# Threshold attention and a squared-ReLU layer on one core: thresholds on ScalarE, first loads over two queues, values and results on GpSimd's queue

## The chip, the cores and the metric

The kernel runs on one core of a Trainium2 chip. The metric is device time in microseconds (us); lower is better. Single executions of the kernel before took between 1449.8 and 1459.9 us over the whole study, so kernels are compared by several executions of each, taken in turn on the same chip.

## The reference, cut to what matters

```python
scores = scale * np.matmul(q, k.transpose(0, 1, 3, 2))          # 8 batches x 8 heads, 576 x 64
thresh = np.max(scores, axis=-1, keepdims=True) - tau
scores = np.where(scores >= thresh, scores, -1000000000.0)
attn = softmax(scores)                                            # written out in the reference
x = (attn @ v) laid out as (4608 tokens, 512)
h = x @ w_in;  r = np.maximum(h, 0.0);  out = (r * r) @ w_out     # 512 -> 2048 -> 512, all fp32
```

## The kernel before

The program is recorded in a fixed order for each engine. It walks over 36 "visits" (a pair of heads each) in 160 steps. A step multiplies a block of scores on TensorE (into two score tiles of two banks of TensorE's result memory each, with no second copy, so that VectorE must have read a bank before the next scores go in), takes the row maximum, adds the threshold, exponentiates on ScalarE, masks and sums on VectorE, and divides on GpSimd. The attention weights are then transposed: by TensorE in the first 11 visits, later by VectorE in blocks of 32 and 48 small DMAs per visit (`by_dma`). In between, `fill` deals out pieces of the two layers (`mlp_in`, `product`) of 1.76 us of TensorE work each. A `product` has work that must follow it (additions on VectorE, the store of the result), which is recorded after the next piece.

```python
def load_qk(n):
    for x, t in zip(rows_of(n), (q, k)):
        queue = nc.scalar if n == 0 and t is k else nc.sync
        for m in range(4): ...                      # 4 loads of q, 6 of k, runs of 128 bytes

def load_v(n):
    for u in range(2):                              # 128x4x64 and 64x64 per head
        nc.sync.dma_start(out=t[:, at:at + NBLK, :], in_=...)
        nc.sync.dma_start(out=t[u * D:(u + 1) * D, at + NBLK, :], in_=...)

def scores(s):
    ...                                             # matmuls into sc[u]
    mx, thr = (st[:, j, 0:n] for j in range(2))
    for u in range(n):
        nc.vector.tensor_reduce(out=mx[:, u:u + 1], in_=sc[u][:, :, 0:HALF], axis=AX.XY, op=ALU.max)
    nc.vector.tensor_scalar(out=thr, in0=mx, scalar1=ntau8, scalar2=None, op0=ALU.add)

def exponents(vis, i):
    nc.scalar.activation(out=bias, in_=mx, func=AF.Copy, scale=-SCALE)
    for u in range(len(sc)):
        nc.scalar.activation(out=w[:, u, :]..., in_=sc[u]..., func=AF.Exp, bias=bias[:, u:u + 1], scale=SCALE)

def threshold(vis, i):                              # masks, sums, frees the score banks
    for u in range(n):
        nc.vector.scalar_tensor_tensor(out=wu, in0=sc[u]..., scalar=thr[:, u:u + 1], in1=wu,
                                       op0=ALU.is_ge, op1=ALU.mult, accum_out=sm[:, u:u + 1])
    ...

def place_blocks(vis, pair):                        # 16 issues; three times per visit
    for qb in range(4):
        for j in range(4):
            nc.sync.dma_start(out=to[...], in_=wb[rows, j::4, :, :]...)

def store_rows(j, t0, t1):
    nc.sync.dma_start(out=out[...], in_=osb[:, t0:t1, :])
# ... cuts: rounding of the weights, transposes, the layers, the main loop
```

Of the kernel before, what the change touches and what calls it, by code (L numbers as in the profile page):

```python
# [11 lines left out]
AF = mybir.ActivationFunctionType  # L12
ALU = mybir.AluOpType
# [6 lines left out]
def kernel(  # L20
# [10 lines left out]
    nc = tc.nc  # L31
    B, H, S, D = q.shape
    d_model, d_ff = moe_w_in.shape
    n_tokens = out.shape[0]
    P = 128
    HP = H // 2
    NPAIR = B * HP
    NBLK = S // P
# [18 lines left out]
    ntau8 = const.tile([P, 1], FP32, name="ntau8")  # L57
# [21 lines left out]
    at = RAW * 2 * WP  # L79
# [18 lines left out]
    osb = const.tile([P, 2, d_model], FP32, name="osb")  # L98
# [48 lines left out]
    def rows_of(n):  # L147
        return rows_in[n % 2 if n <= 2 * HP else 0]

    def load_qk(n):  # L150


        b, h = divmod(visits[n][0], HP)
        h *= 2
        for x, t in zip(rows_of(n), (q, k)):
            queue = nc.scalar if n == 0 and t is k else nc.sync
            for m in range(4):
                src = t[b, h + m // 2, :, (m % 2) * 32:(m % 2) * 32 + 32].rearrange("(c p) d -> p c d", p=32)
                last = REST // 32 if t is k and m >= 2 else 0
                to = x[m * 32:(m + 1) * 32, :, :]  # L160
                queue.dma_start(out=to[:, last:, :], in_=src[:, 0:S // 32 - last, :])  # L161
                if last:
                    queue.dma_start(out=to[:, 0:last, :], in_=src[:, S // 32 - last:, :])  # L163

    def load_v(n):
        b, h = divmod(visits[n][0], HP)
        h *= 2
        t = vs[n % 2]
        for u in range(2):
            at = u * (NBLK + 1)  # L170
            nc.sync.dma_start(out=t[:, at:at + NBLK, :],
                              in_=v[b, h + u, 0:NBLK * P, :].rearrange("(c p) d -> p c d", p=P))
            nc.sync.dma_start(out=t[u * D:(u + 1) * D, at + NBLK, :], in_=v[b, h + u, NBLK * P:S, :])

    def prep(n):

# [9 lines left out]
    def scores(s):  # L186

        vis, i = steps[s]
        n = 2 if i < NBLK else 1
        sc = [psum.tile([P, 2, 512], FP32, tag=f"s{u}", name=f"s{u}") for u in range(n)]  # L190
        halves = [(half, u) for half in range(2) for u in range(n)]
        if early():
            halves.sort(key=lambda x: x[1])
        for half, u in halves:
            if i < NBLK:
                rows, lhsT = slice(u * D, (u + 1) * D), qT[u * D:(u + 1) * D, i * P:(i + 1) * P]
            else:
                rows, lhsT = slice(0, P), qmid
            nc.tensor.matmul(sc[u][:, half, 0:HALF], lhsT, kT[rows, half * HALF:(half + 1) * HALF],  # L199
                             start=True, stop=True)  # L200
        st = pool.tile([P, 7, 2], FP32, tag="st", name="st", bufs=4)
        mx, thr = (st[:, j, 0:n] for j in range(2))
        for u in range(n):
            nc.vector.tensor_reduce(out=mx[:, u:u + 1], in_=sc[u][:, :, 0:HALF], axis=AX.XY, op=ALU.max)  # L204
        nc.vector.tensor_scalar(out=thr, in0=mx, scalar1=ntau8, scalar2=None, op0=ALU.add)

        w = w_slots[(s - first_dma) % (2 if by_dma(vis) else 3)][:, 0:n, :]
        weights[vis, i] = w, sc, st

    def exponents(vis, i):  # L210
        w, sc, st = weights[vis, i]
        mx, bias = (st[:, j, 0:len(sc)] for j in (0, 2))
        nc.scalar.activation(out=bias, in_=mx, func=AF.Copy, scale=-SCALE)  # L213
        for u in range(len(sc)):
            nc.scalar.activation(out=w[:, u, :].rearrange("p (h k) -> p h k", h=2), in_=sc[u][:, :, 0:HALF],  # L215
                                 func=AF.Exp, bias=bias[:, u:u + 1], scale=SCALE)
# [174 lines left out]
    def mlp_out(j, f):  # L391

        if f == 0:
            used["o"] = [take("mm", (6, 7)) for t in range(2)]
        o = used["o"]
        for t in range(2):
            mov = wo[:, Q00:Q01 + 1:Q01 - Q00, f, :] if f < HF else wo[:, Q10:Q11 + 1, f - HF, :]
            nc.tensor.matmul(o[t].rearrange("p (h d) -> p h d", h=2), g[:, f, t * P:(t + 1) * P], mov,  # L398
                             start=(f == 0), stop=(f == NFT - 1))
        if f < NFT - 1:  # L400
            return []

        def store():
            for t in range(2):
                nc.scalar.copy(osb[:, t, :], o[t])
            store_rows(j, 0, 2)
        return [store]

    def store_rows(j, t0, t1):
        lo = j * TCH  # L410
        nc.sync.dma_start(out=out[lo + t0 * P:lo + t1 * P, :].rearrange("(t p) d -> p t d", p=P), in_=osb[:, t0:t1, :])



# [2 lines left out]
    def product(j, x, half):  # L417

        if x == 0 and half == 0:
            a, c, b = ring3[2], ring3[0], ring3[1]  # L420
            used["abc"] = a, b, c
            ring3[:] = [b, a, c]
        a, b, c = (bank[y][:, 0:HD] for y in used["abc"])
        p = PRODUCTS[x]
        g0, g1 = g[:, 0:HF, :], g[:, HF:, :]
        left, slot, to = {
            "1": (g0[:, :, 0:P], Q00, a), "5": (gsum[0], FT1, c), "6": (gsum[1], FT2, b), "2": (g1[:, :, 0:P], Q10, a),
            "7": (gsum[0], FT3, b), "4": (g1[:, :, P:], FT4, a), "3": (gsum[1], Q11, c)}[p]
        for f in range(half * HF // 2, (half + 1) * HF // 2):
            nc.tensor.matmul(to, left[:, f, :], wo[:, slot, f, :], start=(f == 0), stop=(f == HF - 1))  # L430
        if not half:
            return []

        def halves(fn):
            for lo in (0, HF // 2):
                fn(slice(lo, lo + HF // 2))

        def then():
            add, sub, tt, u = ALU.add, ALU.subtract, nc.vector.tensor_tensor, u_sum
            if p == "1":  # L440
                nc.scalar.copy(p1s, a)
            elif p == "5":
                halves(lambda f: tt(out=gsum[0][:, f, :], in0=g0[:, f, 0:P], in1=g0[:, f, P:], op=sub))  # L443
            elif p == "6":
                tt(out=u, in0=b, in1=p1s, op=add)  # L445
                tt(out=osb[:, 0, HD:], in0=c, in1=u, op=add)
                halves(lambda f: tt(out=gsum[1][:, f, :], in0=g1[:, f, 0:P], in1=gsum[1][:, f, :], op=sub))
            elif p == "2":
                tt(out=osb[:, 0, 0:HD], in0=a, in1=p1s, op=add)  # L449
            elif p == "7":  # L450
                tt(out=u, in0=b, in1=u, op=add)
                tt(out=osb[:, 1, HD:], in0=c, in1=u, op=add)
            elif p == "4":
                tt(out=osb[:, 1, 0:HD], in0=u, in1=a, op=sub)
                store_rows(j, 1, 2)
            else:
                tt(out=osb[:, 0, HD:], in0=c, in1=osb[:, 0, HD:], op=add)
                store_rows(j, 0, 1)
        return [then]


# [8 lines left out]
    def by_dma(n):  # L470

        return n >= 3 * HP - 1
# [21 lines left out]
    chunk_at, j = {}, 0  # L494
# [3 lines left out]
            j += 1  # L498
    PIECE_US = 1.76
    waiting = deque()  # L500
    state = {"us": 0.0, "left": 0.0, "step": 0, "rounded": 0, "then": []}

    def early():
        return state["step"] < min(chunk_at)
# [24 lines left out]
        return best  # L529

    def after():
        for fn in state["then"]:
            fn()
        state["then"] = []

    def fill(us):
        state["left"] += us
# [10 lines left out]
    pieces, left = [], n_pieces  # L548
    for s, (n, i) in enumerate(steps):
        if s < HP * FIRST:  # L550
            x = int(n > 0 and i == 0)
        else:
            x = 2 if n >= 2 * HP and i == NBLK else 1
# [19 lines left out]
    for s in range(END + 1):  # L573
        state["step"] = s
        on = s < NST
        now = []
        if on:
            n, i = steps[s]
            at = visits[n][1].index(i)
            last = at == len(visits[n][1]) - 1  # L580
            now = list(range(done, done + pieces[s]))
            done += pieces[s]
            more = n + 1 < len(visits)
            short = n < 2 * HP
            if short and at == 0 and 0 < n + 1 < 2 * HP:
                load_qk(n + 2)
            elif not short and at == 1 and more:
                load_qk(n + 1)
            if now:
                round_weights(now[0], 0)  # L590
            scores(s)
# [6 lines left out]
        if on:  # L598
            if at_once:
                exponents(n, i)  # L600
            if lay:
                prep(n + 1)
            elif now:
                round_weights(now[0], 1)
                round_weights(now[0], 2)
# [4 lines left out]
        if 0 < s <= NST and by_dma(steps[s - 1][0]):  # L610
            m, x = steps[s - 1]
# [25 lines left out]
        if on:  # L637
# [8 lines left out]
            elif last and more and n >= 2 * HP:  # L646
                load_v(n + 1)
    after()
    assert not waiting


# [30 lines left out]
```

## Time and profile before

| | before |
|---|---|
| device time, median of 3 | 1455.95 us (1454.76 to 1457.42) |
| the profiled execution | 1450.02 us, span 1448.2 us |
| TensorE busy | 1387.1 us, 96% of the span |
| VectorE / ScalarE / GpSimd busy | 62% / 29% / 43% |
| DMA issues on SyncE's queue | 1,764; full from 290 to 1280 us |

 "Clock" below is the granted clock: the share of TensorE's full speed that the profile shows as allowed; half clock is 0.5.

Names in all views: PE is TensorE, DVE VectorE, ACT ScalarE, POOL GpSimd, SPq SyncE's DMA queue. L199 is a line of the kernel; in the changed kernel most lines have moved by one (L199 to L200, L227 to L228, L318 to L319, L430 to L431).

### The profile page before, as it was taken

To read this page: it belongs to the slowest core of one execution; us is meant where nothing else is said; L and a number is where in the kernel's file an instruction comes from. 1 tells how busy PE (TensorE), PEld (TensorE's weight loads), DVE (VectorE), ACT (ScalarE), POOL (GpSimd) and SP (SyncE) were. 2 spreads that over 40 slices of the span, in tenths; PEclk is the share of its full clock that TensorE was granted. 3 is DMA by queue.
4 is the path that set the end of the run, shared out by engine and by line. 5 is a ranking of instruction groups with operands and counts; after the bars stand their busy time and mean duration, and the time that the engine had idled before them with its cause. 6 is when DMAs were issued, how large, how long until landed. Compare 5 with 4: busy or idle time off the path is not lost.

```text
span 1448.2 us, 22131 instructions
## 1 busy us (share of the span) xinstructions
PE 1387.1 (96%) x7412; PEld 1058.0 (73%) x7412; DVE 904.5 (62%) x1930; ACT 423.1 (29%) x904; POOL 623.9 (43%) x794
## 2 busy tenths in 40 slices
PE   5898888999999999999999999999999999999998
PEld 3676555747787777777777777777777777788887
DVE  5899886568766676666675767666667666631011
ACT  3666554223222322222322222222222222210100
POOL 3588765425343444343343435343434352422321
PEclk9899999999999999999999999999999999999999
DMA  7564442345445545545455454555554445440000
GB/s 149 119 140 109 112 112 52 55 84 96 85 96 91 109 85 96 88 92 88 97 96 105 84 96 85 95 89 100 95 101 84 89 90 91 90 81 19 5 15 15
DMA packets 532528, 125.94 MB, mean 87 GB/s; under 512 B 523712, under 2 KB 523712, under 8 KB 532416
## 3 DMA queue, kind: packets, MB, share of 16 engines
q1 hardware_dynamic: 529984, 124.24, 44.7%
q8 instruction: 60, 0.98, 0.3%
q10 hardware_dynamic: 2400, 0.30, 0.2%
q14 instruction: 52, 0.43, 0.1%
q0 software_dynamic: 32, 0.00, 0.0%
HBM read 48.63 MB, written 9.44 MB: 40 GB/s over the span
## 4 chain that ended last, share of the span: by engine, by line
PE 65%; SPq 20%; DVE 6%; issue 3%; DMA 2%; ACT 2%; POOL 1%; DVEq 0%; ACTq 0%; POOLq 0%
PE bank L367 26%; PE bank L430 16%; SPq L299 12%; PE s L199 9%; PE bank L318 8%; SPq L306 5%; PE bank L398 3%; SPq L161 3%; DVE st L204 2%; PE bank L257 1%; SPq L163 1%; DVE w L227 1%; DVE turned L288 1%; DMA vs<-in_v_dram 1%; DVE turned L138 1%
## 5 line engine op out<-in xcount | busy, mean ns | idle before, releaser
L367 PE MATMUL bank<-xT,w_in_sb 128*128 128x256 f32 x2304 | 519.8, 382 | 3.5 <-POOL w_in_sb L144 2.4
L367 PEld LDWEIGHTS bank<-xT,w_in_sb 128*128 128x128 f32 x2304 | 431.6, 190 | 84.2 <-issue 21.3
L204 DVE TENSOR_REDUCE st<-s 128x1 f32<-128x576 f32 x288 | 206.7, 753 | 296.9 <-PE s L199 296.9
L378 POOL TENSOR_TENSOR g<-g 128x512 f32<-128x512 f32 x144 | 149.8, 1042 | 232.2 <-ACT g L377 209.4
L239 POOL TENSOR_SCALAR w<-w,st 128x576 f32<-128x576 f32 x269 | 236.4, 888 | 31.2 <-DVE st L230 25.2
L227 DVE SCALAR_TENSOR_TENSOR w<-s,st,w 128x576 f32<-128x576 f32 x269 | 207.3, 803 | 52.2 <-ACT w L215 51.9
L430 PE MATMUL bank<-wo,gsum 128*128 128x256 f32 x1024 | 234.2, 382 | 2.9 <-DVE u_sum L445 1.6
L430 PEld LDWEIGHTS bank<-wo,gsum 128*128 128x128 f32 x1024 | 192.5, 190 | 38.6 <-issue 7.6
L199 PE MATMUL s<-kT,qT 64*128 64x288 f32 x1024 | 176.8, 438 | 30.4 <-DVE kT L178 10.3
L237 POOL TENSOR_SCALAR st<-st 128x2 f32<-128x2 f32 (+1 forms) x160 | 38.7, 242 | 379.7 <-DVE w L227 366.1
L215 ACT ACTIVATE w<-s,st 128x576 f32<-128x576 f32 x269 | 186.1, 738 | 12.1 <-ACT st L213 0.4
L318 PE MATMUL bank<-wT,vs 128*64 128x128 f32 (+3 forms) x1700 | 179.7, 358 | 8.7 <-DMA wT<-turned 3.5
L430 PE MATMUL bank<-wo,g 128*128 128x256 f32 x768 | 178.7, 383 | 2.9 <-DVE osb L449 2.9
L199 PEld LDWEIGHTS s<-kT,qT 64*128 64x128 f32 x1024 | 101.1, 190 | 95.2 <-issue 71.4
L288 DVE STREAM_TRANSPOSE turned<-w 128x576 f32<-128x576 f32 x225 | 163.0, 758 | 10.1 <-DMA wT<-turned 3.8
L430 PEld LDWEIGHTS bank<-wo,g 128*128 128x128 f32 x768 | 143.8, 190 | 32.4 <-issue 8.2
L318 PEld LDWEIGHTS bank<-wT,vs 128*64 128x64 f32 x1700 | 107.9, 141 | 78.1 <-issue 25.6
L377 ACT ACTIVATE g<-bank 128x512 f32<-128x512 f32 x144 | 86.3, 599 | 200.7 <-PE bank L367 200.7
L213 ACT ACTIVATE st<-st 128x2 f32<-128x2 f32 (+1 forms) x160 | 33.2, 208 | 328.2 <-DVE st L204 327.5
L332 ACT COPY xT<-bank 128x256 f32<-128x256 f32 x42 | 15.7, 373 | 287.9 <-PE bank L318 287.9
L443 DVE TENSOR_TENSOR gsum<-g 128x512 f32<-128x512 f32 x32 | 20.8, 681 | 107.3 <-PE bank L430 107.3
L398 PE MATMUL bank<-wo,g 128*128 128x512 f32 x128 | 62.0, 619 | 7.3 <-POOL wo L144 7.0
(66 smaller groups left out, 858.1 us busy)
## 6 DMA issues: line engine op xcount, KB each, us to landing
wT<-turned SPq DMA_DIRECT2D x800, 72.0 KB, 2.2
ql<-in_q_dram SPq DMA_DIRECT2D x128, 72.0 KB, 2.5
vs<-in_v_dram SPq DMA_DIRECT2D x72, 128.0 KB, 2.5
wo<-in_moe_w_in_dram SPq DMA_DIRECT2D x16, 512.0 KB, 4.5
wo<-in_moe_w_out_dram SPq DMA_DIRECT2D x16, 512.0 KB, 3.6
out_dram<-osb SPq DMA_DIRECT2D x32, 256.0 KB, 2.3
kl<-in_k_dram SPq DMA_DIRECT2D x62, 72.0 KB, 2.6
wT<-turned SPq DMA_DIRECT2D x200, 20.0 KB, 1.9
```

Of the source, the lines that this page charges most:

```text
L199: nc.tensor.matmul(sc[u][:, half, 0:HALF], lhsT, kT[rows, half * HALF:(half + 1) * HALF], start=True, stop=True)
L204: nc.vector.tensor_reduce(out=mx[:, u:u + 1], in_=sc[u][:, :, 0:HALF], axis=AX.XY, op=ALU.max)
L215: nc.scalar.activation(out=w[:, u, :].rearrange("p (h k) -> p h k", h=2), in_=sc[u][:, :, 0:HALF], func=AF.Exp, bias=bias[:, u:u + 1], sca ...
L227: nc.vector.scalar_tensor_tensor(out=wu, in0=sc[u][:, :, 0:HALF], scalar=thr[:, u:u + 1], in1=wu, op0=ALU.is_ge, op1=ALU.mult, accum_out=s ...
L239: nc.gpsimd.tensor_scalar(out=w[:, u, :], in0=w[:, u, :], scalar1=z[:, u:u + 1], scalar2=rcp[:, u:u + 1], op0=ALU.add, op1=ALU.mult)
L288: nc.vector.transpose(wb[:, u * KB:(u + 1) * KB, i % 2, :], w[:, u, :].rearrange("p (k q) -> p k q", q=32))
L299: nc.sync.dma_start(out=to[:, :, at:at + 64], in_=wb[rows, j::4, :, :].rearrange("p c u q -> p c (u q)"))
L318: nc.tensor.matmul(ps[u * D:(u + 1) * D, 0:nq], vs[n % 2][:, u * (NBLK + 1) + c, :], wT[:, cw, cols], start=(c == 0), stop=(c == NBLK))
L367: nc.tensor.matmul(h[:, x % 2, :], w_in_sb[:, c, f * P:(f + 1) * P], xT[:, c, at:at + TCH], start=(c == 0), stop=(c == NMC - 1))
L378: nc.gpsimd.tensor_tensor(out=to, in0=to, in1=to, op=ALU.mult)
L398: nc.tensor.matmul(o[t].rearrange("p (h d) -> p h d", h=2), g[:, f, t * P:(t + 1) * P], mov, start=(f == 0), stop=(f == NFT - 1))
L430: nc.tensor.matmul(to, left[:, f, :], wo[:, slot, f, :], start=(f == 0), stop=(f == HF - 1))
```

## The change

Intent: to take the threshold addition off VectorE, to get the first q and k in sooner, and to relieve SyncE's queue of the value loads of the DMA-transposed visits and of the results. Results are held back by one piece of work so that GpSimd does not stand waiting for VectorE's additions.

```diff
 def load_qk(n):
-        for x, t in zip(rows_of(n), (q, k)):
-            queue = nc.scalar if n == 0 and t is k else nc.sync
+        for x, t in list(zip(rows_of(n), (q, k)))[::-1]:
             for m in range(4):
+                queue = nc.scalar if n == 0 and m % 2 else nc.sync
 def load_v(n):
+        queue = nc.gpsimd if by_dma(n) else nc.sync
-            nc.sync.dma_start(...)                 # both loads
+            queue.dma_start(...)
 def scores(s):
-        nc.vector.tensor_scalar(out=thr, in0=mx, scalar1=ntau8, scalar2=None, op0=ALU.add)
 def exponents(vis, i):
         nc.scalar.activation(out=bias, in_=mx, func=AF.Copy, scale=-SCALE)
+        nc.scalar.activation(out=thr, in_=mx, func=AF.Identity, bias=ntau8)
 def store_rows(j, t0, t1):
-        nc.sync.dma_start(...)
+        nc.gpsimd.dma_start(...)
 def product(j, x, half):
-                store_rows(j, 1, 2)
+                return [lambda: store_rows(j, 1, 2)]     # and the same for rows 0 to 1
 def after():
+        now = state["last"]
+        state["last"] = []
         for fn in state["then"]:
-            fn()
+            state["last"] += fn() or []
         state["then"] = []
+        for fn in now:
+            fn()
```

The built programs show that TensorE's order of instructions is the same in both, instruction by instruction. So the start times of the 7,412 matmul records of two traces (each matmul of the program leaves two) can be laid side by side, and the difference read at any point.

More of the change, by code (lines that the diff above doesn't have):

```diff
@@ L168, in load_v @@
         t = vs[n % 2]
+        queue = nc.gpsimd if by_dma(n) else nc.sync
         for u in range(2):
             at = u * (NBLK + 1)
-            nc.sync.dma_start(out=t[:, at:at + NBLK, :],
+            queue.dma_start(out=t[:, at:at + NBLK, :],
                               in_=v[b, h + u, 0:NBLK * P, :].rearrange("(c p) d -> p c d", p=P))
-            nc.sync.dma_start(out=t[u * D:(u + 1) * D, at + NBLK, :], in_=v[b, h + u, NBLK * P:S, :])
+            queue.dma_start(out=t[u * D:(u + 1) * D, at + NBLK, :], in_=v[b, h + u, NBLK * P:S, :])
     def prep(n):
@@ L201, in scores @@
         st = pool.tile([P, 7, 2], FP32, tag="st", name="st", bufs=4)
-        mx, thr = (st[:, j, 0:n] for j in range(2))
+        mx = st[:, 0, 0:n]
         for u in range(n):
             nc.vector.tensor_reduce(out=mx[:, u:u + 1], in_=sc[u][:, :, 0:HALF], axis=AX.XY, op=ALU.max)
-        nc.vector.tensor_scalar(out=thr, in0=mx, scalar1=ntau8, scalar2=None, op0=ALU.add)
         w = w_slots[(s - first_dma) % (2 if by_dma(vis) else 3)][:, 0:n, :]
@@ L211, in exponents @@
         w, sc, st = weights[vis, i]
-        mx, bias = (st[:, j, 0:len(sc)] for j in (0, 2))
+        mx, thr, bias = (st[:, j, 0:len(sc)] for j in range(3))
         nc.scalar.activation(out=bias, in_=mx, func=AF.Copy, scale=-SCALE)
+        nc.scalar.activation(out=thr, in_=mx, func=AF.Identity, bias=ntau8)
         for u in range(len(sc)):
@@ L410, in store_rows @@
         lo = j * TCH
-        nc.sync.dma_start(out=out[lo + t0 * P:lo + t1 * P, :].rearrange("(t p) d -> p t d", p=P), in_=osb[:, t0:t1, :])
+        nc.gpsimd.dma_start(out=out[lo + t0 * P:lo + t1 * P, :].rearrange("(t p) d -> p t d", p=P), in_=osb[:, t0:t1, :])
     PRODUCTS = ("1", "5", "6", "2", "7", "4", "3")
@@ L454, in then @@
                 tt(out=osb[:, 1, 0:HD], in0=u, in1=a, op=sub)
-                store_rows(j, 1, 2)
+                return [lambda: store_rows(j, 1, 2)]
             else:
                 tt(out=osb[:, 0, HD:], in0=c, in1=osb[:, 0, HD:], op=add)
-                store_rows(j, 0, 1)
+                return [lambda: store_rows(j, 0, 1)]
         return [then]
@@ L500 @@
     waiting = deque()
-    state = {"us": 0.0, "left": 0.0, "step": 0, "rounded": 0, "then": []}
+    state = {"us": 0.0, "left": 0.0, "step": 0, "rounded": 0, "then": [], "last": []}
     def early():
@@ L531, in after @@
     def after():
+        now = state["last"]
+        state["last"] = []
         for fn in state["then"]:
+            state["last"] += fn() or []
+        state["then"] = []
+        for fn in now:
             fn()
-        state["then"] = []
     def fill(us):
@@ L648 @@
     after()
+    after()
     assert not waiting
```

## The prediction

> **What bounds the kernel now.** I read the busy table of the page first, then the busy times by stretch, then the waits of TensorE in each stretch, and last the queue of SyncE and the single slow threshold instructions in the order of time. The first two (columns: stretch, its length, then busy time and instruction count of each engine, granted clock, share and rate of the DMA engines):
>
> ```profile
> PE 1387.1 (96%) x7412; PEld 1058.0 (73%) x7412; DVE 904.5 (62%) x1930; ACT 423.1 (29%) x904; POOL 623.9 (43%) x794
> ...
> 0.00:36.00 36.00, 18.41 (x74) 12.81 (x76) 20.77 (x46) 12.06 (x24) 11.69 (x23) 0.91 0.79 149
> 36.00:252.00 216.00, 189.57 (x1385) 129.94 (x1382) 182.85 (x378) 129.97 (x290) 150.88 (x174) 0.96 0.45 108
> 252.00:1290.00 1038.00, 1024.48 (x5236) 780.95 (x5235) 684.18 (x1473) 265.54 (x565) 421.28 (x562) 1.00 0.50 91
> 1290.00:1448.00 158.00, 154.59 (x723) 134.33 (x721) 16.67 (x33) 15.58 (x29) 40.07 (x36) 1.00 0.06 18
> ```
>
> TensorE is the bound. Its idle time, the most that this change can win since no matmul is removed, is 17.6 us in the head, 26.4 us in the early stage (216 - 189.6; first batch, weights being rounded), 13.5 us in the long steady stage (1038 - 1024.5) and 3.4 us at the end: 61 us, or 4.2% of the span. The waits of TensorE, for 36 to 252 us and then for 252 to 1290 us (columns: us in total, times, longest):
>
> ```profile
> PE bank L398 <- POOL wo L144: 7.0, 5, 2.6
> PE s L199 <- DVE wo L227: 6.4, 4, 2.3
> PE s L199 <- DVE w L227: 6.0, 6, 2.0
> ```
>
> ```profile
> PE bank L318 <- DMA wT<-turned: 3.5, 4, 1.7
> PE bank L430 <- DVE osb L449: 2.9, 2, 1.9
> PE bank L430 <- DVE u_sum L445: 1.6, 1, 1.6
> PE s L199 <- DVE kT L178: 1.4, 3, 0.6
> ```
>
> Early, the score matmuls wait for VectorE to free their banks (12.4 us together) and the second layer waits for rounded weights (7.0, and 2.4 more for the first layer's). Later, the value matmuls wait for transposed weights that arrive by DMA, and the products for VectorE's additions. The SyncE queue in the steady stage shows why those DMAs are late:
>
> ```profile
> 699.97 9.81 SPq L299 DMA_DIRECT2D wT<-turned  x15
> 709.87 0.55 SPq L411 DMA_DIRECT2D out_dram<-osb  x1
> 710.46 0.44 SPq L171 DMA_DIRECT2D vs<-in_v_dram  x1
> 710.95 0.57 SPq L173 DMA_DIRECT2D vs<-in_v_dram  x1
> 711.56 0.59 SPq L171 DMA_DIRECT2D vs<-in_v_dram  x1
> 712.19 0.52 SPq L173 DMA_DIRECT2D vs<-in_v_dram  x1
> 712.81 11.16 SPq L306 DMA_DIRECT2D wT<-turned  x16
> ```
>
> Each entry begins where the one before it ends. From 290 to 1280 us (990 us) its DMA issues alone take 917 us and no gap between two issues exceeds 0.36 us: the queue is full, at about 0.6 us an issue, and values and results stand in line with the transposed weights.
>
> **What the skill says.** (1) "DMA: Bandwidth & Descriptors", section "Issuing engines are not separate DMA queues": a second issuing engine saves only issue time, usually small. Here issue time is what has run out on SyncE, so this case is the exception; the DMA engines themselves are half busy (0.50 above). (2) Same page, "SWDGE vs HWDGE vs iDMA": transfers started by GpSimd have their descriptors written by its own cores in software. The trace has one, 0.77 us of GpSimd's time for 0.5 KB (shown below); none of the size now moved, so its cost is my largest unknown. (3) "SBUF — State Buffer", section "Who interferes with whom": a tensor_scalar of VectorE in a two-port mode and a GpSimd instruction exclude each other for the whole instruction. The trace agrees: the threshold addition has a median of 228 ns and a mean of 359, and its slow cases end with GpSimd's instruction (the addition at 31.14 us lasts to 31.95, GpSimd's to 31.92). (4) "ScalarE: Activation LUTs", section "Table sets: the hidden batching unit": identity is in every set. So no second table load is due; the trace before has one load, though Exp, Relu and Copy alternate, and the built program has no further load either.
>
> ```profile
> 1.45 0.77 POOL L58 DMA_DIRECT2D ntau<-in_tau_dram  x1
> 30.65 1.27 POOL L144 TENSOR_TENSOR w_in_sb<-turned 128x512 f32<-128x512 f32 x1
> 31.14 0.81 DVE L205 TENSOR_SCALAR st<-st,ntau 128x2 f32<-128x2 f32 x1
> ...
> L205 DVE TENSOR_SCALAR st<-st,ntau 128x2 f32<-128x2 f32 (+1 forms) x160 | 57.5, 359 | 5.7
> ```
>
> The order of TensorE's instructions is the same in both programs; ScalarE gets 160 activations more, VectorE 160 fewer, and 134 DMA issues go from SyncE to GpSimd (100 for values, 34 for results).
>
> **Part 1, thresholds.** VectorE loses 160 x 359 ns = 57.5 us, of which 15.7 us in 32 instructions lie in the early stage. ScalarE gets 160 x about 208 ns (the mean of the like-sized negated maximum) = 33 us, placed between bias and exponents, so every exponent comes 0.2 us later. What counts is which of the two the masking instruction waits for. In the early stage it starts with no idle time on VectorE ahead of it in all but the steps at 13.8, 26.9, 33.3, 64.5 and 244 us: VectorE is the later one, with 0.3 to 2 us to spare. Not all 15.7 us is won. Where a weight-rounding instruction follows (also a tensor_scalar), it inherits the wait for GpSimd, so those steps win the bare 0.22 us; only the three slow cases followed by a transposition (0.8, 1.3, 1.3 us) win more. That is 31 x 0.22 + 0.58 + 1.08 + 1.08 = 9.6 us of VectorE time in the early stage. The score matmuls were late in about half of the early steps (idle time on TensorE ahead of them), so I take half, 4.8 us, off the 21.8 us of waits named. Three steps in which ScalarE is the later one lose 3 x 0.2 = 0.6. Net **-4.2 us**. In the steady stage five waits for VectorE's additions (5.7 us) shorten by about 0.3 us each, as the addition stands behind one attention step: **-1.5 us**.
>
> **Part 2, first loads.** Before, SyncE issues four q loads by 2.8 us and goes on to the second pair's at 3.5, while ScalarE still issues k until 5.3 (six issues with gaps); k's last piece is followed by its transposition at 8.13 us and the first matmul at 8.97. Afterwards each queue has five issues at about 0.5 us from 0.74 us, so all ten are out by some 3.5 us and none shares the DMA engines with the second pair. With 2.5 to 3 us to land, q's transposition can start at about 6.2, k's follows at 7.0, the first matmul at about 7.8: **-1.2 us**, passed on whole because the first steps are one serial chain.
>
> **Part 3, queues.** SyncE loses 100 x 0.56 us and 34 x 0.47 us = 72 us of issue time, 7% of its steady stage. Transposed weights then land some 2 to 3 us earlier per visit, more than the longest wait (1.7). I remove the 3.5 us plus the 1.1 us in the same row with no named releaser: **-4.5 us**. Holding a result back by one piece keeps GpSimd from waiting for the addition. GpSimd gets at least 134 x 0.77 = 103 us, from 43% to 50%; four issues in a row, 3 to 4 us per visit of 41 us. A stall arises only where this block falls just before the last square of a chunk: from that square to the product that needs its sum are 5.2 us of TensorE work (three half products of 1.73) against 0.6 + 1.04 + 1.04 = 2.7 us of work, so 2.5 us to spare. A hit costs 1 to 2 us; some 6 of each 65 us are exposed, 25 blocks, hence two or three hits: **+3 us**, since other GpSimd work adds to it. The last result leaves by GpSimd instead of SyncE (0.39 us issue, 2.3 us to landing): **+1 us** at the very end.
>
> Sum: -4.2 - 1.5 - 1.2 - 4.5 + 3 + 1 = -7.4 us, so 1455.95 - 7.4 = about **1448.5 us**.
>
> **Rivals.** *GpSimd becomes late.* A value load is 512 rows of 256 B, and if software needs 3 us for each instead of 0.8, a block is 10 us and nearly every one near a chunk's end stalls the products; 25 x 1 us and the delayed division of the weights would give 1465 to 1490. For it: the only example in the trace is tiny. Against it: 57% of GpSimd is idle and weights have four steps (33 us) from division to use. *SyncE was the true pace-maker.* It is as full as TensorE; freed, all of the 13.5 us of steady idle time and the early gain go: 1438 to 1442. Against it: several of those waits are for VectorE. *The longer ScalarE chain counts in full.* 35 early steps x 0.2 = +7 us with no win on VectorE: about 1456. For it: this row of VectorE's waits.
>
> ```profile
> DVE w L227 <- ACT w L215: 51.9, 44, 3.3
> ```
>
> Against it: all but about five of the 44 lie after 240 us, where TensorE has other work.
>
> **Range and chances.** The best case is bounded: winning half of all 61 idle us, which needs everything to go right, just reaches 2% (29 us). The slow side hangs on one unmeasured cost. 8 in 10: 1436 to 1460 us. Faster by over 2%: 0.03; within 2%: 0.92; slower by over 2%: 0.05.
>
> **What would show it.** First score matmul near 7.8 us; the row of TensorE's waits for transposed weights nearly gone and gaps appearing in SyncE's queue; fewer waits for the masking instruction between 36 and 252 us; on GpSimd about 0.8 us per issue and at most a few us of TensorE waiting for squares or their sums. I am wrong if a value load costs GpSimd 2 us or more, if new waits of TensorE for GpSimd exceed 10 us, or if the early stage does not shorten.

## More of the kernel before

The profiled execution was 5 to 7 us quicker than the timed ones.

The line below gives the shares of the chain of work that ended last, by engine. "SPq" is SyncE's queue: a fifth of the chain's time goes from one of its DMA issues to the next.

```profile
PE 65%; SPq 20%; DVE 6%; issue 3%; DMA 2%; ACT 2%; POOL 1%; DVEq 0%; ACTq 0%; POOLq 0%
```

## The result, and the profile after

The changed kernel took 1434.01 us (median of 4, 1431.16 to 1436.05) beside 1456.62 us for the kernel before: 22.6 us, ratio 0.9845 (95% interval 0.9822 to 0.9868). The predicted range ended at 1436: wrong, on the side of too little gain.

The busy table and the table by stretch of the changed kernel (stretch, length, busy time and count of PE, PEld, DVE, ACT, POOL, then granted clock, DMA share and rate; its span ends at 1434.0):

```profile
PE 1383.4 (96%) x7412; PEld 1055.1 (74%) x7412; DVE 853.3 (60%) x1770; ACT 435.5 (30%) x1064; POOL 708.4 (49%) x928
...
0.00:36.00 36.00, 18.94 (x80) 12.98 (x81) 19.32 (x43) 12.68 (x28) 11.97 (x24) 0.91 0.75 149
36.00:252.00 216.00, 193.28 (x1400) 133.91 (x1399) 176.34 (x346) 131.62 (x321) 156.09 (x182) 0.95 0.45 109
252.00:1290.00 1038.00, 1032.26 (x5290) 787.65 (x5288) 641.00 (x1349) 278.27 (x692) 504.55 (x688) 1.00 0.50 92
```

TensorE's idle time in the steady stage fell from 13.5 to 5.7 us (1038 - 1032.3), in the early stage from 26.4 to 22.7. GpSimd's busy time rose by 84.5 us, VectorE's fell by 51. TensorE's waits in the early stage, then in the steady one:

```profile
PE bank L399 <- POOL wo L144: 7.0, 5, 2.6
PE s L200 <- DVE w L228: 6.0, 6, 1.7
PE s L200 <- DVE wo L228: 4.7, 4, 2.1
```

```profile
PE bank L431 <- DVE osb L450: 2.1, 2, 1.4
PE bank L431 <- DVE u_sum L446: 1.4, 1, 1.4
PE bank L368 <- ACT osb L406: 1.2, 1, 1.2
PE s L200 <- DVE kT L179: 0.8, 2, 0.4
```

The row of waits for transposed weights (3.5 us before, and 1.1 without a named releaser) is gone; and the waits for GpSimd that I feared are not there: the steady stage's list has none, and the early one's 7.0 us for rounded weights are the same as before. SyncE's queue and GpSimd's issues around the same place as the stretch shown in the prediction:

```profile
695.44 3.25 SPq L300 DMA_DIRECT2D wT<-turned  x5
698.79 11.24 SPq L307 DMA_DIRECT2D wT<-turned  x16
710.07 1.67 SPq L161 DMA_DIRECT2D kl<-in_k_dram  x3
```

```profile
693.64 0.82 POOL L172 DMA_DIRECT2D vs<-in_v_dram  x1
694.47 0.54 POOL L174 DMA_DIRECT2D vs<-in_v_dram  x1
695.00 0.81 POOL L172 DMA_DIRECT2D vs<-in_v_dram  x1
695.79 0.54 POOL L174 DMA_DIRECT2D vs<-in_v_dram  x1
```

The values no longer stand between two batches of transposed weights; one visit's cost GpSimd 2.7 us. Between 290 and 1270 us SyncE's issues now take 847 us instead of 901, and 24 gaps of over 0.5 us make 67 us, where there were 3 of together 3 us: the queue has air. The chain that ended last says the same in one line:

```profile
PE 86%; DVE 7%; issue 2%; ACT 2%; POOL 2%; DMA 1%; SPq 1%; DVEq 0%; POOLq 0%; ACTq 0%
```

Laid side by side, matmul by matmul, the changed kernel's trace is ahead by 0.5 us at the first matmul, by 3.6 at 280 us, by 7.4 at 640 and by 15.7 at the last; then it loses 1.4 us, since 5.4 us instead of 4.0 pass from the last matmul's start to the end. That is 14.2 us between two traces, and 22.6 us between the timed runs. Two questions follow: which part gave what, and where the other 8 us are. By arithmetic, they are 6.6 us by which the traced execution of the kernel before lies under its median (1456.62 - 1450.02) and 1.7 us by which that of the changed kernel lies over its own (1435.75 - 1434.01).

### The profile page after: what moved, and what is told of

Same layout as the page of the kernel before. It is cut to its first block, busy times and chain, and to the rows that moved or that the text cites. A ratio compares the mean times of both kernels' runs of the same rounds, so it can differ in the third digit from the quotient of the medians. Undisturbed runs are those within 1.5% of the kernel's fastest.

```text
span 1434.0 us, 21996 instructions
## 1 busy us (share of the span) xinstructions
PE 1383.4 (96%) x7412; PEld 1055.1 (74%) x7412; DVE 853.3 (60%) x1770; ACT 435.5 (30%) x1064; POOL 708.4 (49%) x928
## 4 chain that ended last, share of the span: by engine, by line
PE 86%; DVE 7%; issue 2%; ACT 2%; POOL 2%; DMA 1%; SPq 1%; DVEq 0%; POOLq 0%; ACTq 0%
PE bank L368 35%; PE bank L431 23%; PE s L200 12%; PE bank L319 11%; PE bank L399 3%; DVE w L228 1%; DVE st L205 1%; DVE turned L138 1%; PE bank L258 1%; DVE turned L137 1%; DVE turned L289 1%; ACT wT L259 1%; DVE turned L140 0%; DVE wo L228 0%; DMA wo<-in_moe_w_in_dram 0%
```

## The experiments

Eighteen runs in five groups (some repeat a kernel), each group on one chip with its own runs of the kernel before; all gave correct outputs. Gains in us are (1 - ratio) times the median of the kernel before in that group.

| kernel | median us | before, same group | ratio (95% interval) | gain us |
|---|---|---|---|---|
| before again | 1456.1 | 1454.7 | 1.0014 (0.9999 to 1.0029) | -2.0 |
| thresholds only | 1445.7 | 1454.7 | 0.9945 (0.9927 to 0.9963) | 8.0 |
| first loads only | 1453.6 | 1454.7 | 1.0001 (0.9981 to 1.0020) | -0.1 |
| queues only | 1446.6 | 1454.7 | 0.9950 (0.9937 to 0.9964) | 7.3 |
| thresholds and first loads | 1443.0 | 1454.3 | 0.9928 (0.9905 to 0.9951) | 10.5 |
| the change, values back on SyncE | 1436.8 | 1454.3 | 0.9882 (0.9859 to 0.9905) | 17.2 |
| the change, results back on SyncE | 1431.1 | 1454.3 | 0.9841 (0.9817 to 0.9866) | 23.1 |
| the change again | 1432.1 | 1454.3 | 0.9850 (0.9824 to 0.9876) | 21.8 |
| the change, results not held back | 1432.6 | 1455.1 | 0.9843 (0.9829 to 0.9857) | 22.8 |
| the change, values by ScalarE | 1598.5 | 1455.1 | 1.0984 (1.0968 to 1.1000) | -143 |

The theories. *Queue relief*: SyncE's queue was full, and most of the gain is the issue time taken off it. *Vector relief*: the thresholds gave most, in the steady stage too. *A lucky trace*: the first profile was quicker than a usual execution.

**The kernel before, again.** No edit.

> The unchanged kernel, run as if it were a change. If the first profile of it (1448 us) was a lucky execution, as the timed runs at 1455 to 1457 suggest, this profile has a span of 1452 to 1458 us and waits of TensorE for transposed weights of 8 us or more (3.5 before) between 252 and 1290 us. If instead timed runs simply take longer than profiled ones, it repeats 1448 us and 3 to 5 us of those waits. Ratio 1.000 within 0.2%.

Its trace has a span of 1449.8 us and 4.8 us of waits for transposed weights (and 1.2 unnamed): neither case as stated, nearer the second. The two traced executions took 1450.0 and 1451.6 us, the five untraced ones of this run 1454.3 to 1456.9. But quick executions without a trace occur too: of the 60 for this kernel, 6 took 1451.6 us or less, the quickest 1449.8. So both traces are of quick executions and show less than a usual run loses; that tracing itself makes them quick is not shown.

**Thresholds alone.**

```diff
-        nc.vector.tensor_scalar(out=thr, in0=mx, scalar1=ntau8, scalar2=None, op0=ALU.add)
+        nc.scalar.activation(out=thr, in_=mx, func=AF.Identity, bias=ntau8)
```

> Thresholds on ScalarE alone. Theory 'queue relief' (most of the gain is issue time taken off SyncE): 1 to 4 us faster, nearly all before 252 us, and the waits for transposed weights stay. Theory 'vector relief' (VectorE's 57 us less also bring the transposed weights earlier in the steady stage): 8 us or more faster, with those waits halved.

8.0 us: vector relief is right about the size, queue relief about the waits. They did not halve; they grew:

```profile
PE bank L318 <- DMA wT<-turned: 7.4, 7, 1.8
PE bank L318 <- issue: 2.4, 3, 1.8
```

That is 9.8 us against 4.6 in the first trace of the kernel before. In this trace the kernel was 4.6 us ahead of the first trace of before at 120 us, 2.7 at 280 and 0.8 us *behind* at the last matmul. In the steady stage the value matmuls (L318, which need the transposed weights) lost 8.4 us and all others gained 4.9: there, all that VectorE gave was taken back behind SyncE's queue. It was the slowest of its six executions (1450.8 us; the others 1443.5 to 1446.9), so the size is that of one unlucky execution.

**First loads alone.** The `load_qk` part of the diff.

> First loads alone. Both theories: first score matmul 0.5 us earlier, as in the changed kernel (8.45 against 8.97 us), total within 1 us of before. A gain over 2 us would mean that the order k before q in all later loads matters too.

As expected: first score matmul at 8.56 us instead of 8.97, nothing in the total (the order k before q in later loads is worth nothing either). Its trace happened to be slow (span 1457.3 us), and it shows what a slow execution of a kernel with a full SyncE queue looks like. TensorE in the order of time, and then the stretch after the wait:

```profile
659.64 1.24 PE L199 MATMUL s<-kT,qT 64*128 64x288 f32 x8
663.14 3.60 PE L318 MATMUL bank<-wT,vs 128*64 128x256 f32 x20 [2.26 <-DMA wT<-turned]
```

```profile
664.00:667.50 3.50, 3.50 (x17) 2.12 (x13) 0.01 (x1) 0.72 (x2) 0.00 (x0) 0.52 0.61 108
```

TensorE waited 2.26 us for transposed weights. Then its granted clock was 0.52 for 3.5 us: the records show half clock from 664.1 us on, for 3.4 us. The same follows a wait of 1.90 us for one of VectorE's additions, at 766.5 us. So in these two places a wait of about 2 us cost up to 1.7 us more than itself. Not every such wait does: one of 1.91 us at 760 us in the first trace of the kernel before drew no such stretch.

**Queues alone.** The `load_v`, `store_rows`, `product` and `after` parts.

> Values and results by GpSimd's queue, results one piece later, nothing else. 'Queue relief': 12 to 20 us faster, waits for transposed weights in the steady stage under 1 us. 'Vector relief': 5 us or less.

7.3 us, between the two cases. The waits for transposed weights are gone from the trace, and its six executions lie within 2.4 us (1445.8 to 1448.2), those of the kernel before in the group within 6.1. Laid beside the first trace of before it gains 5.8 us between 280 us and the end, and its end is 1.4 us longer. Laid beside the whole change (which adds thresholds and first loads) it is 10.9 us behind at the last matmul: 4.7 of these come before 280 us and 6.2 after. The thresholds are worth as much in the steady stage as in the early one. Of the 6.2 us, 2.9 come before products that wait for VectorE's additions (0.2 to 0.5 us each) and 3.3 before score matmuls: 0.2 to 0.5 us in each of eight places, about 0.06 in fourteen more. Where I looked, at 345, 672 and 722 us of the queues-only trace, these score matmuls start 0.1 to 0.2 us after VectorE's masking instruction ends.

**The change again, and three doses of relief.** Without the queue part, 0 us of issue time is off SyncE; with values back on it, 16 us (34 results x 0.47); with results back, 56 us (100 x 0.56); the whole change 72 us.

> The changed kernel again, beside the partial ones on one chip. Ratio to before 0.984 to 0.987 (20 to 23 us), more than the 8 to 9 us of the thresholds alone plus the 7 to 8 us of the queues alone. Its runs should lie closer together than those of kernels whose SyncE queue is full.

> Thresholds and first loads, all values and results still on SyncE: no issue time taken off. If the full SyncE queue swallows part of VectorE's gain, this stays at 8 to 9 us (ratio 0.994) and its trace shows more waits for transposed weights than before's 3.5 to 4.8 us. If the parts simply add, the same, so the proof lies with the next two.

> The change with values back on SyncE (16 us of issue time off instead of 72). 'Full queue': the steady stage needs most of the 72 us, so this gives 10 to 14 us of the 22. 'Any relief will do' (what hurts is the results, which make the queue wait for VectorE's additions): 18 us or more.

> The change with results back on SyncE and at once (56 us of issue time off). 'Full queue': 19 to 22 us. 'Results block the queue': 14 us or less.

In the order of relief (0, 16, 56 and 72 us) the gains are 10.5 (a little over the 8 to 9 expected), 17.2 (neither case), 23.1 and 21.8 us. 16 us of relief already give more than half of what the queue part adds, 56 give all. The whole change gives more than its parts alone (8.0 + 7.3 - 0.1 = 15.2). That its runs lie closer together than those of a kernel with a full queue did not come true: they span 4.0 us, those without the queue part 4.1. Against my "full queue" numbers, which asked for 10 to 14 us at 16 us of relief, the queue needed little air. Nor did results block it: with all of them on SyncE and the values elsewhere nothing is lost, and in the trace with everything on SyncE no result's issue between 290 and 1280 us waits long enough for VectorE's additions to be listed. The waits for transposed weights in the traces are 5.6 us (2.4 named, 3.2 not) with no relief, 0.6 with 16 us, none with 56 or 72. TensorE's waits for transposed weights with no relief:

```profile
PE bank L318 <- issue: 3.2, 5, 1.3
PE bank L318 <- DMA wT<-turned: 2.4, 2, 1.9
```

This pair of traces, without and with the queue part (the first one of the whole change), is the cleanest of all: they agree to 0.05 us from 40 to 520 us, then the whole change draws ahead by 8.4 us up to 1280 us, and 8.0 of these come before value matmuls. Once the values are off the queue, moving the results too is worth nothing, and at the end it costs: 3.9 us from the last matmul to the end with results on SyncE, 5.4 on GpSimd.

**Results not held back.** `after` and `product` as before, the store on GpSimd.

> The change with results on GpSimd's queue but not held back by one piece of work. If GpSimd then stands waiting for VectorE's additions and squares come late: new waits of TensorE behind GpSimd and 3 us or more slower than the 1432 us of the whole change. If GpSimd has slack enough: the same within 2 us.

The same within noise. GpSimd does stand waiting for VectorE's additions, 59 us in the steady stage instead of 6, but nothing on TensorE waits for GpSimd: holding the results back was not needed.

**Values by ScalarE's queue.**

```diff
-        queue = nc.gpsimd if by_dma(n) else nc.sync
+        queue = nc.scalar if by_dma(n) else nc.sync
```

> The change with the later values by ScalarE's queue instead of GpSimd's. If only SyncE's relief counts: 1432 us, as the whole change. If four issues in a row, 2.3 us per visit, hold up the exponents or the evacuation of matmul banks, 2 to 6 us slower, with waits of TensorE or VectorE for ScalarE.

Slower by 143 us, far outside both cases. SyncE's waits and TensorE's, from 252 to 1290 us:

```profile
SPq L300 <- DMA vs<-in_v_dram: 207.4, 23, 12.3
```

```profile
PE bank L319 <- DMA wT<-turned: 102.3, 21, 6.5
```

The transposed weights on SyncE wait for value loads, with which they share no data. The built program shows why, and the trace has the same numbers: SyncE's and ScalarE's loads take turns on eight completion semaphores (100 to 107), and each issue waits for the last load that used the same one. A value load stands in ScalarE's instruction stream behind its exponents and copies, so SyncE's queue stops until ScalarE gets there. GpSimd's DMAs use eight others (108 to 115). TensorE's granted clock is 0.952 here (154 us at half clock in the trace). So the change works because it went to GpSimd's queue; "another queue" would have been a bad way to put it.

**TensorE's clock.** The kernel before had a mean granted clock of 0.990 over its executions in three groups, the changed kernel 0.994 over its thirteen. In all traces so far the first record of full clock comes at 24 to 34 us, with score matmuls at half speed before it, and half clock returns in several stretches of 3.4 or 6.8 us before 210 us. To see what that is worth I gave TensorE matmuls that nobody reads.

```diff
+    def keep_warm(count):                     # 40 at the start, 18 after each of the first two score steps
+        for _ in range(count):
+            nc.tensor.matmul(bank[4][:, 448:512], ident, ident[:, 0:64], start=True, stop=True)
```

> The kernel before with 76 matmuls that nobody reads, of 64 columns, in TensorE's idle time ahead of its first steps; nothing else. In its trace TensorE ran at half clock until about 25 us and in five later stretches (24 us in all). If half-clock time in the head sits on the serial chain of the first steps, the eight score matmuls of each of the first four steps take 1.2 us instead of 2.3 to 3.0, and the total falls by 3 to 6 us (ratio 0.997). If the early stage is VectorE's alone, nothing changes beyond 1 us.

> Thresholds on ScalarE, split first loads, values by GpSimd, results on SyncE at once, and the same 76 idle matmuls. Without them that was 1431.1 us (ratio 0.984). If the idle matmuls help the two kernels alike: 1425 to 1428 us (ratio 0.980 to 0.982); if half-clock time was what the change itself had removed, no further gain here.

Both failed in either case: 1471.7 us (ratio 1.0112) for the kernel before with them, and 1449.9 (0.9962) for the change with results on SyncE. Each of these took longer than I had reckoned, and they did not lift the clock:

```profile
1.37 17.33 PE L568 MATMUL bank<-ident 128*128 128x64 f32 x80 [1.37 <-POOL ident masks.py:199]
18.63 2.30 PE L199 MATMUL s<-kT,qT 64*128 64x288 f32 x8
```

After 17 us without a pause the eight records of the first score matmuls still take 2.30 us, as at 8.97 us in the first trace; the first record of full clock comes at 43.6 us. Next, few but wide ones (512 columns): four at the start, three after each of the first two score steps.

> The kernel before with ten matmuls of 512 columns that nobody reads, ahead of the first three score steps. The narrow idle matmuls (64 columns) kept TensorE occupied for 27 us and the next score matmuls still took 2.30 us, so occupancy alone does not bring the full clock. If what counts is the share of columns streamed, the eight score matmuls of steps 1 to 3 now take about 1.2 us and the total is 2 to 5 us shorter; if the clock of the head depends on something else (time since start), they stay at 2.3 us and the total is 0 to 4 us longer.

> Thresholds, split loads, values by GpSimd, results on SyncE at once, with the same ten wide matmuls. First case: 1426 to 1429 us, 2 to 5 under the same kernel without them. Second case: 1431 to 1435. If half-clock time in the early stage is what varies between runs, this kernel's runs also lie closer together.

Now the clock was full from 10.1 us on and the first eight score matmuls took 1.25 us, though they came late, at 11.8 us, because the zeros for the idle matmuls were set by VectorE behind its wait for tau. The kernel before won 3.5 us by the medians (1451.96 against 1455.43, ratio 0.9975), as expected; the other won nothing clear (1430.4, 0.9832, the same ratio as without them), and its runs do not lie closer together (1429.8 to 1434.1). The wide matmuls differ from the narrow ones in their data too (zeros, where the narrow ones multiply the identity), in number and in start; which of these counts was not separated.

> Results on SyncE at once, values on GpSimd: again, beside the whole change on the same chip. Its end is 1.5 us shorter in the traces (3.9 us from the last matmul instead of 5.4), so 1 to 2 us faster than the whole change if nothing else differs; if the results' 16 us of issue time matter, slower.

> The whole change, for that comparison: 1430 to 1434 us, ratio 0.984 to 0.986.

1431.07 us (0.9832) against 1434.32 us (0.9844): results on SyncE are better by 1.7 us (0.0012 x 1455.4) in the means, in the expected direction and size; the two intervals overlap.

Last, in two kernels with results on SyncE: zeros set by GpSimd at the start, so that the wide matmuls begin at 1.8 us; and in the second kernel three more of them before steps 3 and 5.

> As best_wide, but the zeros for the wide idle matmuls are set by GpSimd at the start, so that these begin near 2 us instead of 6.3 (there they waited behind VectorE's wait for tau and delayed the first score matmul from 8.5 to 11.7 us). If full clock from the first score on is worth what best_wide hid: first score matmul at 8.5 us lasting 1.25 us for eight, step 3 about 3 us earlier than without (27.0 us), total 1427 to 1429 us. If the early stage gives it back later: 1430 to 1432.

> The same with three more wide matmuls in the gaps before steps 3 and 5, to remove the half-clock stretch at 27 to 34 us. If that stretch costs, 1 to 2 us faster than best_early; if the added matmuls stand in the way of the score matmuls, 1 to 2 us slower.

1428.0 us (0.9825) and 1424.3 us (0.9803, interval 0.9790 to 0.9817), beside 1453.0 us for the kernel before. The first is as expected, but its ratio is within noise of the same kernel without wide matmuls (0.9832, on another chip); the second gained more than the 1 to 2 us expected. The second beats the change: its executions of 1423.2 to 1424.8 us lie below all of the changed kernel's (1430.5 and up, on other chips). Its trace is at full clock from 6.7 us on, but for one stretch of 3.4 us at 194.5 us:

```profile
18.16 1.94 PE L202 MATMUL s<-kT,qT 64*128 64x288 f32 x8 [0.23 <-DVE wo L230]
...
23.40 1.94 PE L202 MATMUL s<-kT,qT 64*128 64x288 f32 x8 [0.44 <-DVE w L230]
```

In the changed kernel the matching score matmuls begin at 20.2 and 27.0 us.

## Why the prediction was wrong, point by point

**What bounds the kernel** was right: TensorE, with SyncE's queue full beside it. The limit of 61 us of idle time held too: 14 us were won between the traces, 22.6 between the timed runs. The reading of the queue was a little too clean: from 290 to 1280 us the trace has 908 us of issues, not 917, and seven gaps of over 0.36 us, the longest 4.0 us at 1277. The reading of the slow threshold additions holds: all 35 of over 0.3 us end within 0.12 us of a GpSimd instruction's end. As foreseen, the changed kernel still has one table load.

**First loads, -1.2 us**: mis-sized. The first matmul came 0.2 to 0.5 us earlier in the traces and alone the part gives nothing measurable. The ten issues were out by 4.2 us, not 3.5: the last two on each queue took 1.6 and 1.9 us together, most of it a pause before the last one.

**Thresholds, early stage, -4.2 us**: about right. 3.1 us between the first pair of traces from the first matmul to 280 us, 4.7 us (0.5 of it the first matmul's) between queues-only and the whole change; two later traces of the whole change give 4.5 and 6.4 us beside the same trace of before, with less half clock in this stage than the first. The wait for the masking instruction fell only from 12.4 to 10.7 us, as ScalarE is now the later one in several steps; the threshold takes ScalarE 285 ns, not the 208 I put in.

**Thresholds, steady stage, -1.5 us**: this is the first step that failed. The traces show 6.2 us there. I had counted only the five named waits for VectorE's additions (5.7 us, of which I took 1.5); 2.9 us were won before those products. The other 3.3 us were won before score matmuls, which I had left out: with one instruction less on VectorE in each step its masking ends sooner and frees the score banks sooner, a few tenths in eight places. The rows of waits name only 0.7 us of these 3.3.

**Queues, -4.5 us**: 5.8 us between the traces of before and queues-only in the steady stage; 8.4 us once VectorE no longer holds the work up, 8.0 of it before the value matmuls. The mechanism was right; the size came from one trace with little waiting. With thresholds alone the waits were 9.8 us, so the part that VectorE gives needs the queue's air. In the timed runs the queue part gives 7.3 us by itself and about 11 on top of the rest (21.8 - 10.5); that difference of 4 us is no larger than the intervals allow, so it is likely, not shown.

**GpSimd late, +3 us**: did not happen. A value load costs GpSimd 0.80 or 0.54 us, as estimated from 0.77, and TensorE never waits for GpSimd in the steady stage. It was counted as a likely cost without a trace that showed one, and is a third step that failed. **The end, +1 us**: 1.4.

**The sum** of -7.4 us stands against -14.2 between the first two traces, and was then subtracted from the timed median of 1455.95 us, though all terms came from a trace of 1450.0 us. This is another step that failed. Most timed runs of the kernel before lose some 4 to 6 us that its traces do not show, while the changed kernel's three traces (1432.8, 1434.4 and 1435.75 us) lie among its timed runs (1430.5 to 1436). The split-only trace shows one way to lose it: waits of about 2 us that each draw a stretch of half clock after them. The mean clocks point the same way: 0.990 against 0.994 is (0.010 x 1453 - 0.006 x 1431) x 2, about 12 us less at half clock, hence up to 6 us of TensorE's work. But that is an upper bound, and likely far too high for half clock in the early stage: two traces of the changed kernel (1435.75 and 1432.8 us) differ there by 17 us of half clock and by only 2.9 us of time. Single executions of the kernel before do not follow their clock closely either (one of 1449.8 us had 0.989). So the cause of these 4 to 6 us stays open: no timed run leaves a trace.

**The rivals.** "SyncE was the true pace-maker" (1438 to 1442) was nearest, and I argued it away by pointing out that several waits are VectorE's: the change relieves both, and in the traces each is worth more with the other (the queue part 8.4 us instead of 5.8, the thresholds 6.2 in the steady stage instead of a loss of 3.5 in the thresholds-only trace, or 3.7 with first loads). "GpSimd becomes late" and "the longer ScalarE chain counts in full" fell.

## What to carry to other kernels

When the limiting engine waits now for one queue and now for another engine, price a relief of one with the other relieved too, and remember that an engine's short instructions delay what comes after them also in places where no wait is listed. Look at more than one execution before pricing waits from a trace, and do not subtract a trace's gains from a timed median that the trace does not match. Before moving DMA issues to another queue, look at which completion semaphores that queue shares; and a few wide matmuls that nobody reads, placed where TensorE idles at the start, were here worth more (some 4 us by the ratios, 0.9803 against 0.9832 on another chip) than a tuned load order (nothing).

## What the Trainium skill lacked or had wrong

- "DMA: Bandwidth & Descriptors", section "Issuing engines are not separate DMA queues": it calls the issue time saved by another engine usually small relative to the DMA itself. Here an issue took about 0.6 us beside 2.2 us to landing (transposed weights), but SyncE's queue was full, and 16 us of issue time off it took the kernel from 10.5 to 17.2 us of gain.
- No page that I read has this: issues of SyncE and ScalarE wait for one another through the eight completion semaphores that this program shares between them. Values on ScalarE's queue stopped SyncE for 207 us and cost 143.
- The same DMA page, section "SWDGE vs HWDGE vs iDMA", gives no cost to GpSimd by size of transfer. Measured: 0.80 us for 512 rows of 256 B, 0.54 for 64 such rows, 0.60 for 128 rows of 2 KB; a value load landed 3.5 us after its issue (median) instead of 2.5 from SyncE.
- "TensorE: Matmul & The Clock Gate", section "Part 1: The HAM clock gate", gives a window of about 3.4 us for the change between half and full clock. The stretches of 3.4 and 6.8 us agree. Lacking: 17 us of 64-column fp32 matmuls without a pause did not lift the clock, 512-column ones (of zeros) from 1.8 us on did by 6.7; and waits of 2.26 and 1.90 us, shorter than a window, were followed by half clock, while one of 1.91 us was not.
